# A packed-attention and channel-mix kernel: the second sequence's k is loaded ahead of w_k and transposed between warm-up products, w_r's first piece is loaded ahead of v, the ninth block of the first weights goes first

## The chip, the cores and the metric

The kernel runs on one core of one Trainium2 chip. The metric is device time in microseconds of one execution, the median of several runs. A profiled execution is looked at beside it: its span is the time from its first to its last instruction, and its own time is the device time of that one execution. The text calls TensorE PE, VectorE DVE, ScalarE ACT, GpSimd POOL and the queue of SyncE, from which nearly all transfers are issued, SP.

## The reference, cut to what matters

```python
scale = 1.0 / np.sqrt(64)                       # q, k, v: (8, 8, 576, 64); p: (8, 8, 32, 64)
def sm_attn(qq, kk, vv):
    s = scale * np.matmul(qq, kk.transpose(0, 1, 3, 2))
    a = np.exp(s - np.max(s, axis=-1, keepdims=True))
    a = a / (np.sum(a, axis=-1, keepdims=True) + 1e-09)
    return np.matmul(a, vv)
p_packed = sm_attn(p, k, v)                     # 32 rows for each head
x = sm_attn(q, p_packed, p_packed)              # then (8, 576, 512): heads side by side
x_prev = x moved down by one row, its first row 0
xk = mu_k * x + (1.0 - mu_k) * x_prev
xr = mu_r * x + (1.0 - mu_r) * x_prev
kk = np.maximum(xk @ w_k, 0.0)                  # w_k (512, 1024), float64, as w_v and w_r
v = kk * kk @ w_v                               # w_v (1024, 512)
out = 1.0 / (1.0 + np.exp(-(xr @ w_r))) * v     # w_r (512, 512)
```

## The kernel before, in words

Eight sequences of 576 rows make 4608 rows of x; the channel mix takes them in nine blocks (NB) of 512 rows. For each block there are three chains of products on PE: the gates (xr @ w_r, written to `pr`), the keys (xk @ w_k, written to `ph`) and the values (squared keys @ w_v, written to `pvo`). Each operand is split into a high and a low part, so every product of 128x128 by 128x512 is done three times, in lines 1206 to 1208, 1158 to 1160 and 1236 to 1238; such a group of three is called a main group below.

The weights are float64 in memory. Each of the 4 pieces of w_r, 8 of w_k and 8 of w_v is loaded into an `st` buffer of 512 KB and converted in `convert`: ACT makes `m` (L297), DVE does three steps on it (L299, L301, L303), ACT casts the high part (L311), DVE subtracts to get the low part (L313).

The first sequence is treated in a way of its own. Its k, v and q are loaded as whole runs (`runs`), k is transposed on PE (L395) and copied by ACT (L398); `first_front` makes the scores (L548), DVE takes the row maxima (L642, L644), ACT the exponentials (`first_weights`, L646 and L651). The weights `a` are transposed in nine blocks (L568) into two PSUM tiles, `copied` brings them to `aT` (L632 for four blocks, L634 for the ninth), and nine times 16 products with v (L582) give the packed values, which DVE scales (`pm`, L600). They are transposed (L611), copied by ACT (`ppB`, L620), and `by_token` makes the second attention's scores with q (L927, L932); `weights_by_token` makes its softmax on DVE and ACT (`et`, lines 949 to 963), its transposes go to `A` (L976). `first_mix` multiplies A by pm, already weighed with mu (L1027), and ACT and DVE write the tiles xr and xk of the first block (L1043, L1052). The second sequence's k and q (`loads`, b < EARLY) are loaded with 96 rows to a tile, `raw`, and transposed on PE in `transposed_on_pe` (L479, six transposes to a pair of heads, 24 for k), ACT copies them (L482), and L670 makes the scores from them. The other sequences are transposed by DVE.

Nothing is ordered by hand. A planner, `Flow`, runs when the program is built: each part of the work is a generator that names the engine and a duration that the planner supposes, and at each step the part that could start first goes next, with its rank as the tie breaker. Ranks also decide who gets a buffer. What the planner decides is a fixed order of instructions on each engine, each queue working strictly in that order. Transfers are put in order by ranks too: `FIRST` holds those of the four pieces of w_r, `lrank` those of a sequence's k, v and q, `RANK_W` that of w_k. While it expects PE to be idle the planner puts in warm-up products, `fill` (L1342, tile `spare`), each of which shows in the trace as two passes; it stops that when the second part of the first block's gates begins. The buffers in play are `sq` (8, first v and q of the first sequence, later tiles of xr and squared keys), `raw` (3), `kq` (4), `st` (8) and two PSUM tiles `pa`.

Of the kernel before, what the change touches and what calls it, by code (L numbers as in the profile page):

```python
# [16 lines left out]
class Flow:  # L17
# [21 lines left out]
    def __init__(self):  # L39
        self.free = {"tensor": 1.4}  # L40
        self.parts = []
        self.n = 0
        self.now = None
        self.when = {}
        self.waiting = {}
        self.slots = {}
        self.table = "exp"
        self.warmth = 0.0
        self.keep_busy, self.fill = 0.0, None
# [73 lines left out]
    def order(self, part):  # L123

        start, ready = self.start(part)
        engine, table = part.want[0], part.want[3]
        if table and table != self.table and start - ready < self.PATIENCE:
            start += self.TABLE
        if part.last == (engine, part.t) and part.gen.__name__ in self.CHAINS:
            start = max(start - self.SAME, self.free.get(engine, 0.0))  # L130
        return start, part.rank, part.n
# [40 lines left out]
def attn_pack_channel_mix(ctx: ExitStack, tc: tile.TileContext, q, k, v, p, mu_k, mu_r, w_k, w_v, w_r, out):  # L172
    nc = tc.nc
# [21 lines left out]
    FIRST = 9.992, 10.06, 10.07, 10.08  # L195
    RANK_1, RANK_MIX, RANK_W, RANK_V, LOADS_1 = 14.28, 11.5, 13.6, 15.2, 14.29
# [69 lines left out]

    warm = const.tile([P, 1], F32, name="warm")
# [58 lines left out]
    def loads(b):  # L326
        flow.spawn(packed(b), lrank(b) - 0.03)
        for src, tag in ((k, "kT"), (v, "vt"), (q, "qT")):
# [7 lines left out]
            flow.now.rank = lrank(b) - (0.02 if tag == "kT" else 0.0)  # L336
            for pr in range(NPR):

                slot = yield from flow.take("raw")
                if b < EARLY:  # L340

                    raw = tile_([P, 6, 2 * D], F32, "raw", slot, "raw")
                    for hh in range(2):
                        yield from load(
                            raw[:T6, :, hh * D:(hh + 1) * D], src[b, 2 * pr + hh].rearrange("(c p) d -> p c d", p=T6),
                            0.5, 0.62,
                        )
                        back_to_issue()
                    flow.spawn(transposed_on_pe(tag, b, pr, slot, raw), rank(b), flow.free["dma"] + LANDS)
                    continue  # L350

# [9 lines left out]
                flow.spawn(transposed(tag, b, pr, slot, raw), rank(b), flow.free["dma"] + LANDS)  # L361

# [106 lines left out]
    def transposed_on_pe(tag, b, pr, raw_slot, raw):  # L469
# [10 lines left out]
        flow.give("raw", raw_slot)  # L480
# [55 lines left out]
    def first_front():  # L536
# [28 lines left out]
        for o, n, copy in ((0, 4, act), (4, 4, act), (8, 1, act)):  # L565
# [10 lines left out]
        for o, n in ((0, 4), (4, 4), (8, 1)):  # L576
            yield from flow.wait(("aT", 0, o), *(("vt", 0, pr) for pr in range(NPR)))
            yield pe(0.13 * n)
            for j in range(o, o + n):
                for pr in range(NPR):  # L580
                    for h, own in enumerate(HALVES):
                        nc.tensor.matmul(  # L582
                            pv[32 * pr:32 * pr + 32, h, :D], aT[own, j, 32 * pr:32 * pr + 32],
                            vts[0, pr][1][own, j * D:(j + 1) * D], start=(j == 0), stop=(j == RUN - 1),
                        )
# [601 lines left out]
    def gates(i):  # L1187

        for tiles in ((0,), (1, 2, 3)) if i == 0 else ((0, 1), (2, 3)) if i == 1 else ((t,) for t in range(NT)):
            slots, prs = [], []  # L1190
            if i == 0:
                yield from flow.wait(*made("xr", i, 0, tiles[0]))
                if tiles[0]:
                    flow.keep_busy = 0.0
                    flow.give("m", 3)
            for x in tiles:
# [26 lines left out]
    def values(i):  # L1223
        slots, pv = {}, {}
        for f in range(NF):
            yield from flow.wait(("sq", i, f), *(("wv", f, o) for o in range(0, DM, WP)))
            sf, hl = sqs.pop((i, f))
            for t in range(NT):
# [7 lines left out]
                nc.tensor.matmul(pv[t], sh, wvs[f][:, 0, :], start=(f == 0), stop=False)  # L1236
                nc.tensor.matmul(pv[t], sh, wvs[f][:, 1, :], start=False, stop=False)  # L1237
                nc.tensor.matmul(pv[t], sl, wvs[f][:, 0, :], start=False, stop=(f == NF - 1))  # L1238
                if f == NF - 1:
                    flow.spawn(done(i, t, slots[t], pv[t]), 0, flow.t + flow.LAG)  # L1240
            flow.give("sq", sf)

    def done(i, t, slot, pv):
        yield from flow.wait(("sig", i, t))
        sg, sig = sigs.pop((i, t))
        yield vec(DM)
# [94 lines left out]
    def fill():  # L1341
        nc.tensor.matmul(spare[:, :P], ident, ident, start=True, stop=True)  # L1342
# [28 lines left out]
```

## Time and profile before

| what | value |
|---|---|
| median of three runs | 591.75 us |
| the profiled execution's own time | 591.73 us |
| its span | 589.6 us |
| PE busy | 579.4 us (98% of the span), 4119 products |
| DVE busy | 371.8 us (63%) |
| ACT busy | 316.4 us (54%) |
| bytes read from and written to HBM | 43.00 MB and 12.98 MB |

Of the three runs 591.61 is the lowest; one, at 1153.4 us, stands apart. The profiled execution's own time is 2.1 us over its span; the table's busy times are of the span. Products are pipelined and the trace's durations of them overlap, so PE's busy time is above the time that it needs; the distance from one start to the next tells that.

### The profile page before, as it was taken

The page shows a single profiled execution, that of the slowest core. Times are in us where ns is not written, and L with a number is a line of the kernel's source. Part 1 is how long each engine was busy: PE and PEld are TensorE (multiplying, and loading weights), DVE is VectorE, ACT ScalarE, POOL GpSimd, SP SyncE. Part 2 cuts the span into 40 slices and gives each one's busy share as a digit, 9 for nine tenths or more (in the row PEclk, how much of TensorE's full clock was granted, in tenths as well). Part 3 has the DMA queues.
Part 4 walks back from the last instruction along what each step waited for, and adds up shares of the span by engine and source line. Part 5 has one row for each costly group of instructions (what it writes and reads, how often), then busy time and mean ns, then how long its engine had stood idle before and what let it go on. Part 6 is the DMA issues. An engine that isn't in the chain of part 4 may idle for free.

```text
span 589.6 us, 10544 instructions
## 1 busy us (share of the span) xinstructions
PE 579.4 (98%) x4119; PEld 457.2 (78%) x4119; DVE 371.8 (63%) x702; ACT 316.4 (54%) x571; POOL 7.8 (1%) x33
## 2 busy tenths in 40 slices
PE   8999999999999999999999999999999999999997
PEld 7877777787687778778778777878788888888885
DVE  1899889856892897289876697379214712541321
ACT  4678984764753692287456475358335613721410
POOL 3000000000000000000000000000000000000000
PEclk9999999999999999999999999999999999999999
DMA  8887340863556176346466444400100010001001
GB/s 304 334 231 238 114 65 10 190 141 59 127 118 146 25 155 139 91 112 138 78 183 135 83 101 117 116 2 0 73 0 1 0 73 0 1 0 72 1 1 71
DMA packets 160593, 56.66 MB, mean 96 GB/s; under 512 B 136856, under 2 KB 150304, under 8 KB 160544
## 3 DMA queue, kind: packets, MB, share of 16 engines
q1 hardware_dynamic: 160224, 55.86, 37.4%
q8 instruction: 32, 0.52, 0.4%
q0 software_dynamic: 320, 0.14, 0.1%
q14 instruction: 17, 0.14, 0.1%
HBM read 43.00 MB, written 12.98 MB: 95 GB/s over the span
## 4 chain that ended last, share of the span: by engine, by line
PE 74%; DVE 16%; ACT 5%; issue 2%; DMA 1%; SPq 1%; DVEq 0%; ACTq 0%
PE ph L1158 10%; PE ph L1159 9%; PE ph L1160 9%; PE pvo L1236 9%; PE pvo L1237 8%; PE pvo L1238 8%; PE pr L1206 5%; PE pr L1208 5%; PE pr L1207 5%; DVE x L1113 2%; PE pa L894 2%; DVE m L301 2%; PE pa L704 1%; DMA q<-in_q 1%; PE pa L670 1%
## 5 line engine op out<-in xcount | busy, mean ns | idle before, releaser
L1158 PE MATMUL ph<-xk,wk_h 128*128 128x512 f32 x288 | 115.5, 401 | 0.0
L1236 PE MATMUL pvo<-wv,sq 128*128 128x512 f32 x288 | 113.9, 396 | 0.0
L1159 PE MATMUL ph<-xk,wk_h 128*128 128x512 f32 x288 | 112.4, 390 | 0.0
L1160 PE MATMUL ph<-xk,wk_l 128*128 128x512 f32 x288 | 112.2, 390 | 0.0
L1237 PE MATMUL pvo<-wv,sq 128*128 128x512 f32 x288 | 112.2, 390 | 0.0
L1238 PE MATMUL pvo<-wv,sq 128*128 128x512 f32 x288 | 112.1, 389 | 0.0
L1169 ACT ACTIVATE r<-ph 128x512 f32<-128x512 f32 x72 | 43.2, 600 | 86.5 <-PE ph L1160 84.4
L1180 DVE CAST sq<-r 128x512 fp32r<-128x512 f32 x64 | 26.9, 421 | 97.1 <-ACT r L1172 93.6
L1236 PEld LDWEIGHTS pvo<-wv,sq 128*128 128x128 f32 x288 | 54.1, 188 | 16.3 <-issue 5.4
L1158 PEld LDWEIGHTS ph<-xk,wk_h 128*128 128x128 f32 x288 | 54.0, 188 | 16.3 <-issue 5.4
L1160 PEld LDWEIGHTS ph<-xk,wk_l 128*128 128x128 f32 x288 | 54.1, 188 | 11.5
L1238 PEld LDWEIGHTS pvo<-wv,sq 128*128 128x128 f32 x288 | 54.1, 188 | 11.4
L1237 PEld LDWEIGHTS pvo<-wv,sq 128*128 128x128 f32 x288 | 54.1, 188 | 10.6
L1159 PEld LDWEIGHTS ph<-xk,wk_h 128*128 128x128 f32 x288 | 54.2, 188 | 10.1 <-DVE xk L1052 0.2
L1206 PE MATMUL pr<-wr_h,xr 128*128 128x512 f32 x144 | 57.5, 399 | 0.3 <-ACT xr L1133 0.3
L1208 PE MATMUL pr<-wr_h,xr 128*128 128x512 f32 x144 | 56.2, 390 | 0.3 <-DVE xr L1135 0.3
L1207 PE MATMUL pr<-wr_l,xr 128*128 128x512 f32 x144 | 56.2, 390 | 0.0
L1113 DVE SCALAR_TENSOR_TENSOR x<-xt,mus,x 128x448 f32<-128x448 f32 (+6 forms) x112 | 52.7, 510 | 4.8 <-ACT x L1107 4.8
L1107 ACT ACTIVATE x<-xt,mus 128x448 f32<-128x448 f32 (+7 forms) x112 | 54.2, 529 | 1.2 <-DVE xr L1135 1.2
L1182 DVE TENSOR_TENSOR sq<-r,sq 128x512 fp32r<-128x512 f32 x72 | 49.2, 683 | 4.7 <-ACT sq L1177 3.3
L1218 ACT ACTIVATE sig<-pr 128x512 f32<-128x512 f32 x36 | 20.9, 600 | 55.3 <-PE pr L1208 55.1
L1247 DVE TENSOR_TENSOR sig<-pvo,sig 128x512 f32<-128x512 f32 x36 | 24.0, 685 | 37.3 <-PE pvo L1238 37.2
(151 smaller groups left out, 707.6 us busy)
## 6 DMA issues: line engine op xcount, KB each, us to landing
out<-sig SPq DMA_DIRECT2D x31, 256.0 KB, 2.6
vt<-in_v SPq DMA_DIRECT2D x14, 512.0 KB, 4.8
raw<-in_k SPq DMA_DIRECT2D x96, 72.0 KB, 2.7
raw<-in_q SPq DMA_DIRECT2D x96, 72.0 KB, 2.7
st<-in_moe_w_k SPq DMA_DIRECT2D x8, 512.0 KB, 8.5
st<-in_moe_w_v SPq DMA_DIRECT2D x8, 512.0 KB, 5.0
far<-at SPq DMA_DIRECT2D x12, 288.0 KB, 2.8
aTd<-far SPq DMA_DIRECT2D x12, 256.0 KB, 3.0
```

The lines of the kernel that those rows point to most:

```text
L1107: nc.scalar.mul(x32[:, o:o + n], xts[b, c][:, 1 + s:1 + s + n], mus[:, j, c:c + 1])
L1113: nc.vector.scalar_tensor_tensor(x32[:, o:o + n], xts[b, c][:, s:s + n], mus[:, j + 1, c:c + 1], x32[:, o:o + n], op0=ALU.mult, op1=ALU.add,)
L1158: nc.tensor.matmul(ph, wk_h[:, c, fs], xh, start=(c == 0), stop=False)
L1159: nc.tensor.matmul(ph, wk_h[:, c, fs], xl, start=False, stop=False)
L1160: nc.tensor.matmul(ph, wk_l[:, c, fs], xh, start=False, stop=(c == NC - 1))
L1182: nc.vector.tensor_tensor(hl[:, 1, :], r, hl[:, 0, :].bitcast(F32), op=ALU.subtract)
L1206: nc.tensor.matmul(pr, xh[:, ts_], wr_h[:, c, :], start=(c == 0), stop=False)
L1207: nc.tensor.matmul(pr, xh[:, ts_], wr_l[:, c, :], start=False, stop=False)
L1208: nc.tensor.matmul(pr, xl[:, ts_], wr_h[:, c, :], start=False, stop=(c == NC - 1))
L1236: nc.tensor.matmul(pv[t], sh, wvs[f][:, 0, :], start=(f == 0), stop=False)
L1237: nc.tensor.matmul(pv[t], sh, wvs[f][:, 1, :], start=False, stop=False)
L1238: nc.tensor.matmul(pv[t], sl, wvs[f][:, 0, :], start=False, stop=(f == NF - 1))
```

## The change

Six edits are made. The planner holds PE free from 0.5 instead of 1.4, and the warm-up products take a tile of zeros, set by DVE at the start, in place of the identity, which POOL makes. The ranks put w_r's first piece ahead of v, and the second sequence's k (`K_1`) ahead of w_k; that k is now loaded into buffers of `sq` rather than `raw` (`whole`). In `first_front` the ninth block is transposed and multiplied first. `copied` is preferred by 0.6 in the planner's choice. The very last main group of the last block is cut into two halves of 256 columns, and so are its multiplication by the gate and its write. Buffer `a` has one slot fewer until the second part of the first gates.

```diff
-        self.free = {"tensor": 1.4}
+        self.free = {"tensor": 0.5}
...
+        if part.gen.__name__ == "copied":
+            start = max(start - 0.6, self.free.get(engine, 0.0))
...
-    FIRST = 9.992, 10.06, 10.07, 10.08
-    RANK_1, RANK_MIX, RANK_W, RANK_V, LOADS_1 = 14.28, 11.5, 13.6, 15.2, 14.29
+    FIRST = 9.985, 10.05, 10.06, 10.07
+    K_1, RANK_1, RANK_MIX, RANK_W, RANK_V, LOADS_1 = 10.08, 14.28, 11.5, 13.6, 15.2, 14.29
...
+    flow.slots["a"].pop()
+    zeros = tile_([P, P], F32, "a", 1, "zeros")
+    nc.vector.memset(zeros, 0.0)
...
+            if b < EARLY:
+                if tag == "kT":
+                    flow.spawn(whole(src, tag, b), K_1)
+                else:
+                    yield from whole(src, tag, b)
+                continue
...
+    def whole(src, tag, b):
+        space = "sq" if tag == "kT" else "raw"
+        for pr in range(NPR):
+            slot = yield from flow.take(space)
+            raw = tile_([P, 6, 2 * D], F32, space, slot, "raw")
+            for hh in range(2):
+                yield from load(
+                    raw[:T6, :, hh * D:(hh + 1) * D], src[b, 2 * pr + hh].rearrange("(c p) d -> p c d", p=T6),
+                    0.5, 0.62,
+                )
+                back_to_issue()
+            flow.spawn(transposed_on_pe(tag, b, pr, space, slot, raw), rank(b), flow.free["dma"] + LANDS)
...
-        for o, n, copy in ((0, 4, act), (4, 4, act), (8, 1, act)):
+        for o, n, copy in ((8, 1, act), (0, 4, act), (4, 4, act)):
...
-        for o, n in ((0, 4), (4, 4), (8, 1)):
+        for o, n in ((8, 1), (0, 4), (4, 4)):
...
+                halves = 2 if i == NB - 1 and t == NT - 1 and f == NF - 1 else 1
+                for o in range(0, DM, DM // halves):
+                    cols = slice(o, o + DM // halves)
+                    nc.tensor.matmul(pv[t][:, cols], sh, wvs[f][:, 0, cols], start=(f == 0), stop=False)
...
+        if halves == 2:
+            for o in range(0, DM, DM // 2):
+                cols = slice(o, o + DM // 2)
+                yield vec(DM // 2)
+                nc.vector.tensor_tensor(sig[:, cols], pv[:, cols], sig[:, cols], op=ALU.mult)
+                yield from load(out[i * TB + t * P:i * TB + t * P + P, cols], sig[:, cols], 0.63, 0.4)
+                back_to_issue()
+            return
...
-        nc.tensor.matmul(spare[:, :P], ident, ident, start=True, stop=True)
+        nc.tensor.matmul(spare[:, :P], zeros, zeros, start=True, stop=True)
```

Line numbers after the change are 12 to 25 higher. The rows that follow give the order of instructions on an engine, before and after; a name is the tile that is written and those that are read.

DVE's first instructions before, up to pm (`mx` the first sequence's row maxima, `m` the first piece of w_r in conversion):

```order
L642 TENSOR_REDUCE mx<-pa 128x1
L644 TENSOR_SCALAR nmx<-mx 128x1
L642 TENSOR_REDUCE mx<-pa 128x1
L644 TENSOR_SCALAR nmx<-mx 128x1
L299 TENSOR_SCALAR m<-m 128x512
L301 SCALAR_TENSOR_TENSOR m<-st,m 128x512
L303 SCALAR_TENSOR_TENSOR m<-st,m 128x512
L594 SCALAR_TENSOR_TENSOR rs<-sm 128x2
L596 RECIPROCAL rs<-rs 128x2
L600 TENSOR_TENSOR pm<-pa,rs 128x256
L313 TENSOR_TENSOR wr_l<-m,wr_h 128x512
```

The same stretch of DVE after:

```order
L271 MEMSET zeros 128x128
L304 TENSOR_SCALAR m<-m 128x512
L654 TENSOR_REDUCE mx<-pa 128x1
L656 TENSOR_SCALAR nmx<-mx 128x1
L654 TENSOR_REDUCE mx<-pa 128x1
L656 TENSOR_SCALAR nmx<-mx 128x1
L306 SCALAR_TENSOR_TENSOR m<-st,m 128x512
L308 SCALAR_TENSOR_TENSOR m<-st,m 128x512
L318 TENSOR_TENSOR wr_l<-m,wr_h 128x512
L606 SCALAR_TENSOR_TENSOR rs<-sm 128x2
L608 RECIPROCAL rs<-rs 128x2
L612 TENSOR_TENSOR pm<-pa,rs 128x256
```

The whole conversion of w_r's first piece now stands ahead of pm, and its first DVE step ahead of the row maxima; the ACT step that it waits for (`m<-st`) moved ahead of the first exponentials likewise.

ACT between the last exponential of the first weights and the copies `ppB`, before (`aT` are the copies of the nine blocks, `t` the PSUM tile of the ninth, `qT` the copies of q's transposes):

```order
L651 ACTIVATE a_215,sm<-pa,nmx 128x64
L417 COPY qT<-pq 128x512
L297 ACTIVATE m<-st 128x512
L417 COPY qT<-pq 128x512
L632 COPY aT_277<-pa 128x512 x2
L417 COPY qT<-pq 128x512 x2
L634 COPY aT_277<-t_276 128x128
L311 CAST wr_h<-m 128x512
L297 ACTIVATE m<-st 128x512 x2
L620 COPY ppB<-pa 64x256 x2
```

The same stretch of ACT after:

```order
L663 ACTIVATE a_216,sm<-pa,nmx 128x64
L316 CAST wr_h<-m 128x512
L429 COPY qT<-pq 128x512
L646 COPY aT_291<-t_290 128x128
L644 COPY aT_291<-pa 128x512 x2
L429 COPY qT<-pq 128x512 x2
L302 ACTIVATE m<-st 128x512
L429 COPY qT<-pq 128x512
L632 COPY ppB<-pa 64x256 x2
```

The ninth block's copy moved from behind four copies of qT to behind one, the first piece's cast moved ahead of all of them, and ahead of `ppB` there stands one step of a conversion instead of two.

PE from the third group of second-attention scores to the third main group, before (`tpt` the transposes of the second attention's weights, `raw` the second sequence's k):

```order
L932 MATMUL s2t<-ppB,qT 64x32 x8
L1342 MATMUL spare<-ident 128x128 x2
L969 MATMUL tpt<-ident,et 128x2x64 x4
L1342 MATMUL spare<-ident 128x128 x3
L1027 MATMUL pa<-A_421,pms 64x192 x16
L1342 MATMUL spare<-ident 128x128 x5
L1206 MATMUL pr<-wr_h,xr 128x512
L1207 MATMUL pr<-wr_l,xr 128x512
L1208 MATMUL pr<-wr_h,xr 128x512
L479 MATMUL pa<-ident,raw 128x96 x3
```

The same stretch of PE after:

```order
L944 MATMUL s2t<-ppB,qT 64x32 x8
L491 MATMUL pa<-ident,raw 128x96 x6
L981 MATMUL tpt<-ident,et 128x2x64 x4
L491 MATMUL pa<-ident,raw 128x96 x6
L1367 MATMUL spare<-zeros 128x128 x7
L1039 MATMUL pa<-A_426,pms 64x192 x16
L981 MATMUL tpt<-ident,et 128x2x64 x4
L1367 MATMUL spare<-zeros 128x128 x2
L1219 MATMUL pr<-wr_h,xr 128x512
L1220 MATMUL pr<-wr_l,xr 128x512
L1221 MATMUL pr<-wr_h,xr 128x512
L491 MATMUL pa<-ident,raw 128x96 x12
```

Twelve of k's 24 transposes now stand ahead of the first main group and twelve right behind it; before, six stood in these early gates and eighteen between the main groups of the first keys. On ACT two copies of kT and the last exponential of the second attention's weights came to stand ahead of the four casts of xr; before, none of the four kT copies stood there. In the whole program 36 warm-up products are left of 43, and 16 of ACT's table loads of 18.

## Rows read from the trace of the kernel before

**Rows 1.** The page's first part: busy time of each engine in us, share of the span, number of instructions.

```profile
PE 579.4 (98%) x4119; PEld 457.2 (78%) x4119; DVE 371.8 (63%) x702; ACT 316.4 (54%) x571; POOL 7.8 (1%) x33
```

**Rows 2.** Busy time by stretch: the stretch, its length, busy us and instructions of PE, PEld, DVE, ACT, POOL, then the granted clock of TensorE, DMA share, GB/s.

```profile
20.00:30.00 10.00, 9.62 (x148) 8.73 (x147) 9.65 (x22) 4.88 (x12) 1.17 (x4) 1.00 0.78 272
30.00:40.00 10.00, 9.91 (x147) 7.92 (x145) 9.72 (x25) 6.59 (x18) 0.00 (x0) 1.00 0.78 208
40.00:50.00 10.00, 10.00 (x159) 7.74 (x160) 9.69 (x22) 8.59 (x18) 0.10 (x1) 1.00 0.86 296
50.00:62.00 12.00, 11.86 (x89) 8.53 (x88) 11.83 (x24) 11.42 (x23) 0.00 (x0) 1.00 0.71 204
62.00:80.00 18.00, 17.53 (x107) 14.09 (x109) 13.38 (x26) 17.21 (x33) 0.00 (x0) 1.00 0.36 89
80.00:113.00 33.00, 32.03 (x261) 23.44 (x253) 32.27 (x58) 20.01 (x44) 0.10 (x1) 1.00 0.39 83
```

**Rows 3.** The same view for the warm-up products alone: busy us and passes of PE and PEld, clock, DMA.

```profile
30.00:40.00 10.00, 2.83 (x20) 2.17 (x18) 1.00 0.78 208
40.00:580.00 540.00, 0.00 (x0) 0.00 (x0) 1.00 0.35 82
```

**Rows 4.** Timeline of the first 21 us, rows of PE, ACT and DVE in order of time: start, us, engine, line, operation, tiles, count, and in brackets the idle time before and what ended it.

```profile
2.43 2.50 PE L1342 MATMUL spare<-ident 128*128 128x128 f32 x10 [2.43 <-POOL ident masks.py:199]
...
9.94 1.50 PE L548 MATMUL pa<-kT,pt 64*32 64x320 f32 x32
10.94 0.82 DVE L642 TENSOR_REDUCE mx<-pa 128x1 f32<-128x640 f32 x1 [10.94 <-PE pa L548]
...
13.57 0.66 PE L411 MATMUL pq<-ident,q 128*128 128x128 f32 x4 [0.16 <-DMA q<-in_q]
13.88 0.21 ACT L651 ACTIVATION_READ_ACCUMULATOR a<-pa,nmx 128x1 f32 x1
...
14.80 0.68 ACT L297 ACTIVATE m<-st 128x512 f32<-128x512 f32 x1
14.84 1.04 PE L568 MATMUL pa<-ident,a 128*128 128x128 f32 x8
15.52 0.43 DVE L299 TENSOR_SCALAR m<-m 128x512 uint32<-128x512 uint32 x1 [2.64 <-ACT m L297]
15.92 1.08 ACT L632 COPY aT<-pa 128x512 f32<-128x512 f32 x2
15.98 0.69 DVE L301 SCALAR_TENSOR_TENSOR m<-st,m 128x512 uint32<-128x512 uint32 x1
16.88 1.09 ACT L417 COPY qT<-pq 128x512 f32<-128x512 f32 x2
17.00 1.66 PE L582 MATMUL pa<-v,aT 64*32 64x64 f32 x144
17.83 0.31 ACT L634 COPY aT<-t 128x128 f32<-128x128 f32 x1
18.70 0.42 DVE L600 TENSOR_TENSOR pm<-pa,rs 128x256 f32<-128x256 f32 x1 [1.03 <-PE pa L582]
19.70 0.75 ACT L620 COPY ppB<-pa 64x256 f32<-64x256 f32 x2
```

**Rows 5.** Transfers: issues of k and v on SP (timeline: start, us, count), time from issue to landing of v's four and, last, of w_k's first piece, issued at 12.83; then the time at which ACT first reads w_k.

```profile
3.16 1.86 SPq L219 DMA_DIRECT2D v<-in_v x4
...
DMA to landing us min/median/max: 6.1/6.5/7.0
...
DMA to landing us min/median/max: 8.2/8.2/8.2
...
33.79 0.69 ACT L297 ACTIVATE m<-st 128x512 f32<-128x512 f32 x1
```

**Rows 6.** Timeline of 50 to 62 us: PE's main groups of the first keys, the transposes of the second sequence's k, that sequence's scores; DVE's low parts of xk; ACT's copies of kT.

```profile
50.10 0.39 PE L1158 MATMUL ph<-xk,wk_h 128*128 128x512 f32 x1
53.78 0.39 PE L1159 MATMUL ph<-xk,wk_h 128*128 128x512 f32 x1
54.24 0.66 PE L479 MATMUL pa<-ident,raw 96*128 96x96 f32 x6
54.68 0.47 PE L1158 MATMUL ph<-xk,wk_h 128*128 128x512 f32 x1
55.45 0.41 PE L479 MATMUL pa<-ident,raw 96*128 96x96 f32 x3
59.94 1.20 PE L670 MATMUL pa<-kT,pt 64*32 64x288 f32 x32
...
52.66 0.48 DVE L1052 TENSOR_TENSOR xk<-pa,xk 128x320 fp32r<-128x320 f32 x1
...
53.45 0.68 ACT L482 COPY kT<-pa 128x576 f32<-128x576 f32 x1
```

**Rows 7.** The end: the last rows of the chain that ended last (start, us, what), the writes by size (count, KB, median us to landing), and a row of warm-up passes at 19.45.

```profile
585.31 0.23 PE pvo L1237
585.54 0.24 PE pvo L1238
585.80 0.69 DVE sig L1247
...
out<-sig SPq DMA_DIRECT2D x31, 256.0 KB, 2.6
out<-sig SPq DMA_DIRECT2D x10, 128.0 KB, 2.4
...
19.45 1.28 PE L1342 MATMUL spare<-ident 128*128 128x128 f32 x10
```

**Rows 8.** Who waited for whom on PE over the whole span: us in total, times, longest; behind it, the row of the same view of 40 to 62 us for a wait of the first keys on DVE.

```profile
PE pa L894 <- DVE a L886: 1.8, 4, 0.8
PE pr L1208 <- DVE xr L1135: 0.3, 1, 0.3
...
PEld ph L1159 <- DVE xk L1052: 0.2, 1, 0.2
```

**Rows 9.** Timeline of 29 to 32 us: the last exponential of the second attention's weights and the four casts of xr on ACT, the first main product on PE.

```profile
29.20 0.42 ACT L954 ACTIVATE et<-et 64x256 f32<-64x256 f32 x1
29.52 0.99 ACT L1043 CAST xr<-pa 128x192 fp32r<-128x192 f32 x4
...
30.55 0.48 PE L1206 MATMUL pr<-wr_h,xr 128*128 128x512 f32 x1
```

## What the change should do to the time

> **What bounds the kernel now.** I read the page's busy shares first, then busy time by stretch, then the timeline of the opening, then the chain of waits at the end. PE is busy 98% of the span [rows 1]; that says little, since warm-up products count and overlapping products count twice. By stretch the reader is to see two regimes [rows 2]. From 113 us on, PE runs main groups back to back, and the waits on PE that the whole span shows are a few us [rows 8]; nothing in the diff touches that part except the very end. Ahead of that DVE decides: from 20 to 62 us it works 40.9 of 42 us, while PE is padded with warm-up products up to 40 us and with none after [rows 3]. From 62 to 80 ACT is full (17.2 of 18) and DVE is not (13.4), from 80 to 113 DVE is full again (32.3 of 33). So the change can gain in three places: how early DVE's full stretch begins, what PE and ACT still have to do between 50 and 62, and the tail. The granted clock is 1.00 in all these rows, the level of 2.4 GHz.
>
> All sums are made against the profiled execution's own time, 591.73 us, of which 589.6 are its span; the median of the runs is 591.75, so the two can be taken as one.
>
> **The opening: 0.4 us earlier.** What starts DVE's full stretch is the chain scores, maxima, exponentials, transposes, products with v, pm, ppB [rows 4]. PE starts its first warm-up product at 2.43, when POOL has made the identity; the zeros come from DVE, idle until 10.94, so k can be transposed up to 1.5 us earlier, and the scores, at 9.94 now, may come near 9. That alone gives nothing, because in the new order the maxima wait on DVE behind the first step of w_r's first piece, and that piece has to land. It takes the place of v in the queue. v's four transfers are issued at 3.16 to 4.6 and land 6.1 to 7.0 us later, that is 9.3 to 11.6, one every 0.77 us for 288 KB [rows 5]. A piece of 512 KB counts as 1.8 of them: 9.3 + 0.8 x 0.77 = 9.9. Then ACT's step (0.68) and DVE's first (0.43) [rows 4] put the maxima at about 11.05, where they stood at 10.94. The exponentials end 3.15 us later as before (13.88 + 0.21 against 10.94), at 14.2.
>
> The gain comes after that. Before, the transposes of the weights stand behind two tiles of q and start at 14.84; now behind one, whose products begin at 13.57 and end at 14.2, so all nine are done by 15.3. ACT then casts w_r (DVE is through its two further steps of 0.7 at 14.4; the cast as long as ACT's other step) until 15.05, copies one qT (0.55), the ninth block (0.31) and the eight others (1.08): 17.0, as before. But the ninth block no longer ends the chain. Before, its copy stood behind two qT and began at 17.83, and the products with v ended at 18.66; now only the last four blocks' 64 of 144 products follow at 17.0, 0.75 us, and pm comes at 17.8 instead of 18.70. Of these 0.9 us half is given back: ACT has two more qT, a conversion step and a fourth qT to do before ppB, 17.0 + 1.1 + 0.68 + 0.55 = 19.3, against 19.70. So 0.4 us. Bounds: with w_r landing where v's first does, 9.3, it is 1.0; where v's last does, 11.6, it is -1.3. I take the middle row's pace.
>
> DVE's work from there to 62 us is the same work in another order, and it has no idle time to give up in which the order could matter; the shift of 0.4 stays.
>
> **Loads moved past each other.** v lands up to 1.4 us later, by 13.0; its first use moves from 17.00 to about 16, so it is covered. The eight loads of k (1.15 MB) pass w_k on SP; their buffers are v's, free only after the products with v at 17.8, so SP holds everything behind them until then. Both directions have room: w_k's first piece lands at 12.83 + 8.2 = 21.0 and is first read at 33.79 [rows 5]; three us later costs nothing. pin, v and q of the second sequence come behind and are not needed before 59 us.
>
> **k's transposes and copies: 1.7 us.** Before, eighteen of the 24 transposes stand between main groups of the first keys. From the first such group at 50.10 to the scores at 59.94 are 9.84 us [rows 6]. By the order eleven main groups lie in them, three products of 0.23 us each from start to start [rows 7], so 7.5. The remaining 2.35 us are transposes with their switches and waits. Now these transposes stand where PE ran warm-up products (by the order, 26 of these from 18 us on before, 16 after) and cost it nothing there. Not all of it is gained, because part of that stretch is DVE's: the fourth low part of xk is made from 52.66 to 53.14, and the group that reads it cannot pass before that [rows 6]. From there to the end of the transposes at 55.65 PE loses 0.6 (53.78 instead of 53.15) and 0.7 (54.24 to 54.68, and 55.45 to 55.65 with a slow start after it): 1.3 us is gained even if DVE is no earlier relative to its own shift. With the new order, in which the four low parts stand in one row on DVE, up to the whole 2.35. Zero is the other bound: if w_k's last low parts, DVE's work, become what every group waits for. I take 1.7, nearer to 1.3 because DVE has next to no idle time there.
>
> ACT must keep up: three copies of kT, 0.68 us each or some 0.54 from start to start (two of aT take 1.08 [rows 4]), leave this stretch (11.4 of 12 us busy) for 25 to 35 us, where ACT has five idle. That is 1.6 us off ACT, which is what the ACT-bound stretch to 80 needs to start 1.7 earlier; DVE has 4.6 idle there. From 80 to 113 DVE's full stretch starts earlier by as much and carries the shift to PE.
>
> **The tail: 0.3 us.** The last product ends at 585.78, DVE's multiplication takes 0.69, then the write [rows 7]. Of half the size the multiplication takes 0.42 (pm's, 128x256 [rows 4]): 0.27 gained. A write of 128 KB lands in 2.4 us, one of 256 KB in 2.6: at most 0.2. The six half products cost between 0.112 each, the distance of warm-up passes of 128 columns (1.28 for ten, the last one's drain included), and 0.23, that is 0.67 to 1.36 instead of 0.68; I take 0.15 more. Sum 0.3, bounds -0.4 and 0.5.
>
> The Trainium skill, TensorE: Matmul & The Clock Gate, section Back-to-back issue gap, gives 262 cycles for 256 columns, an estimate of 0.109 us; by it the six cost nothing and the term is 0.45; no row of before has products of 256 columns. The Trainium skill, DMA: Bandwidth & Descriptors, section Rules for kernel authors, advises against cutting a transfer into two halves since they serialize on the same engines; it speaks of partition halves, but by it the smaller write gains nothing and the term is 0.1; the medians of [rows 7] stand against it with 0.2, and no write here was cut in two.
>
> **After 113 us: nothing, give or take 1.** The orders of all later blocks come out a little different. The waits that could vanish are those of [rows 8]; as many can appear.
>
> Sum: 0.4 + 1.7 + 0.3 = 2.4, so 591.73 - 2.4 = 589.3 us.
>
> **The rivals.**
>
> DVE stays the bound. The transposes leave PE but the main groups only wait for w_k's low parts instead. For it: DVE is busy 11.83 of 12 us. Against it: PE shows a wait on DVE of only 0.2 us there [rows 8], though with the transposes there to fill. It leaves the opening and the tail: 591.0.
>
> The order suits the later stretches too. In the two stretches up to 113 the part of DVE's 4.6 idle us that ACT caused is used, and the waits of [rows 8] go: about 2 us more, 587.2.
>
> Slower: the second attention's chain on ACT. The last exponential of `et` stood at 29.20 and the four casts of xr at 29.52 behind it; the first main product came at 30.55 [rows 9]. In the new order a copy of kT and that exponential stand ahead of the casts, and the exponential waits for a DVE step that now comes behind the second group's maxima, sums and product, five steps and about 2.5 us. Counted through, the casts come near 31.4 and the first main product 1.7 us late. PE makes up for it only if it then runs without a pause, which it did not before (2.8 us of warm-up products between 30 and 40 [rows 3]). If it does not, and DVE bounds 50 to 62 too, the sum is 0.4 + 0.3 - 1.7: 592.7. It decides if the first main product comes after about 32 and the gates end later than 50.1.
>
> The change does not do what it says: k's loads wait for v's buffers and hold SP so long that w_k's later pieces or the transposes come late. The 12 us of room in [rows 5] speak against it; 592 or more.
>
> **How the numbers follow.** Forecast 0.54, DVE stays the bound 0.2, later stretches too 0.13, ACT's chain 0.1, loads late 0.03. The range: the largest terms together (1.0 + 2.35 + 0.5, and 1.0 of the later waits) give 586.9, the smallest without the ACT rival (0.4 + 0 - 0.4, and 0.5 of new waits) 592.2; I widen the low end to 586.7. That leaves out about a tenth, half of it above. 2% of this time, 11.8 us, is about what a measurement of this kernel can tell from no change; nothing here comes near it: faster by more 0.01, within 0.98, slower by more 0.01.
>
> **What would show it.** The maxima on DVE start between 10.6 and 11.5, pm's multiplication near 17.8, ppB's copies near 19.3. No kT copy on ACT after 40 us, and the second sequence's scores on PE near 58 instead of 59.94. PE's last product ends about 2 us earlier than at 585.78. I am wrong if w_r's first piece lands after 11, if PE shows waits for w_k's low parts between 52 and 62, or if the shift at 60 us is there and gone at 115.

## The result, and the profile after

The changed kernel takes 595.52 us, the median of five runs (593.7 to 596.11), the kernel before 591.61 in the runs beside it: a ratio of 1.0061, with an interval of 1.0051 to 1.0072. It is slower by 3.9 us where 2.4 us less were forecast, and outside the range. The profiled execution is the quickest of the five, 593.7 us with a span of 591.6; what its trace shows, 2.0 us more than before, is about half of the loss; the four slower executions left no trace.

Busy time by stretch, as in [rows 2], of the changed kernel (columns: stretch, its length, busy time of PE, its weight loads, DVE, ACT and POOL with instructions, granted clock, DMA share, GB/s):

```profile
20.00:30.00 10.00, 9.73 (x152) 8.96 (x151) 9.72 (x23) 5.47 (x10) 0.00 (x0) 1.00 0.94 266
30.00:34.70 4.70, 2.32 (x22) 1.61 (x14) 4.44 (x13) 3.03 (x8) 0.00 (x0) 1.00 1.03 293
36.00:40.00 4.00, 4.00 (x55) 2.19 (x54) 2.08 (x4) 2.13 (x5) 0.00 (x0) 0.57 0.79 226
40.00:50.00 10.00, 9.72 (x161) 7.02 (x153) 7.98 (x19) 7.70 (x19) 0.00 (x0) 1.00 1.01 289
50.00:62.00 12.00, 12.00 (x126) 9.89 (x108) 11.63 (x23) 10.43 (x22) 0.10 (x1) 1.00 0.53 164
```

DVE, which was full from 20 to 62 us in [rows 2], has idle time now: 2.08 of 4 us busy from 36 to 40, 7.98 of 10 from 40 to 50. In the same place PE has 2.4 us without work (30 to 34.7), and behind it the granted clock averages 0.57 for four microseconds, that is, PE runs at 1.2 GHz for most of them. Neither is in the kernel before.

The opening went better than forecast. Timeline of DVE and ACT of the changed kernel, beside [rows 4]:

```profile
9.94 0.82 DVE L654 TENSOR_REDUCE mx<-pa 128x1 f32<-128x640 f32 x1
...
17.96 0.42 DVE L612 TENSOR_TENSOR pm<-pa,rs 128x256 f32<-128x256 f32 x1 [3.12 <-PE pa L594]
...
19.01 0.74 ACT L632 COPY ppB<-pa 64x256 f32<-64x256 f32 x2
```

The maxima start 1.0 us earlier than before, pm and ppB 0.7. What follows is PE from 30 to 41 us; it answers to [rows 9], where the first main product came at 30.55:

```profile
30.95 0.47 PE L1219 MATMUL pr<-wr_h,xr 128*128 128x512 f32 x1
...
32.13 0.44 PE L491 MATMUL pa<-ident,raw 96*128 96x96 f32 x3 [0.25 <-issue]
34.76 0.93 PE L491 MATMUL pa<-ident,raw 96*128 96x96 f32 x9 [2.19 <-DMA raw<-in_k]
35.48 0.48 PE L1219 MATMUL pr<-wr_h,xr 128*128 128x512 f32 x1
...
37.55 0.63 PE L1220 MATMUL pr<-wr_l,xr 128*128 128x512 f32 x1
...
38.54 2.31 PE L1039 MATMUL pa<-A,pms 32*64 32x256 f32 x96
```

Behind the first main group stand twelve transposes of the second sequence's k, the third and the fourth pair of heads in turn, three at a time. The third pair's first three run; the next three belong to the fourth pair, and its data is still on its way: 2.19 us of waiting for `raw`. So all nine that are left, and every main product behind them, wait. ACT stands in the same line: the copies of kT wait for the transposes, and w_r's cast stands behind them:

```profile
32.28 1.24 ACT L302 ACTIVATE m<-st 128x512 f32<-128x512 f32 x2
35.49 1.18 ACT L494 COPY kT<-pa 128x576 f32<-128x576 f32 x2 [1.98 <-PE pa L491]
37.07 0.27 ACT L988 COPY A<-tpt 128x128 f32<-128x128 f32 x1 [0.40 <-PE tpt L981]
37.23 0.62 ACT L316 CAST wr_h<-m 128x512 fp32r<-128x512 f32 x1
```

DVE then waits 2.0 us for that cast. A product of 512 columns that takes 0.39 us elsewhere takes 0.60 to 0.79 from 36.0 to 38.5.

Why the pair is late is seen on SP, which issues the transfers in its fixed order (start, us, what, count); the second fence is the view of that line from 26.8 to 27.8 us, the time from issue to landing of the two loads there, of which the trace holds the landing of the second:

```profile
17.77 6.93 SPq L221 DMA_DIRECT2D raw<-in_k  x6
24.75 1.97 SPq L221 DMA_DIRECT2D st<-in_moe_w_k  x2
26.82 0.93 SPq L221 DMA_DIRECT2D raw<-in_k  x2
```

```profile
DMA to landing us min/median/max: 7.4/7.4/7.4
```

Six of k's eight loads go out together, then two pieces of w_k of 512 KB each, then the fourth pair's two loads, issued at 26.8 and 27.2, the second of which needs 7.4 us to land, up to 34.6. The DMA engines are busy meanwhile (share 1.03 from 30 to 34.7).

### The profile page after: what moved, and what is told of

It reads as the page before. It is cut to its first block, busy times and chain, and to the rows that moved or that the text cites. A ratio compares the mean times of both kernels' runs of the same rounds, so it can differ in the third digit from the quotient of the medians.

```text
span 591.6 us, 10533 instructions
## 1 busy us (share of the span) xinstructions
PE 579.2 (98%) x4108; PEld 455.6 (77%) x4108; DVE 370.7 (63%) x704; ACT 315.4 (53%) x569; POOL 7.8 (1%) x33
## 4 chain that ended last, share of the span: by engine, by line
PE 76%; DVE 12%; ACT 6%; DMA 3%; issue 2%; SPq 0%; DVEq 0%; ACTq 0%
PE ph L1170 9%; PE pvo L1253 9%; PE ph L1172 9%; PE ph L1171 9%; PE pvo L1255 9%; PE pvo L1254 9%; PE pr L1219 5%; PE pr L1221 5%; PE pr L1220 5%; DVE x L1125 2%; PE pa L716 2%; PE pa L906 1%; DMA q<-in_q 1%; DMA raw<-in_k 1%; PE pa L682 1%
## 5 line engine op out<-in xcount | busy, mean ns | idle before, releaser
L1192 DVE CAST sq<-r 128x512 fp32r<-128x512 f32 x64 | 26.8, 419 | 105.9 <-ACT r L1184 103.3
L1219 PE MATMUL pr<-wr_h,xr 128*128 128x512 f32 x144 | 58.0, 403 | 0.0
L1221 PE MATMUL pr<-wr_h,xr 128*128 128x512 f32 x144 | 56.9, 395 | 0.9 <-DVE xr L1147 0.6
L1184 ACT ACTIVATE r<-r 128x512 f32<-128x512 f32 x72 | 45.5, 632 | 1.8
```

The lines of the kernel that those rows point to most:

```text
L1219: nc.tensor.matmul(pr, xh[:, ts_], wr_h[:, c, :], start=(c == 0), stop=False)
L1221: nc.tensor.matmul(pr, xl[:, ts_], wr_h[:, c, :], start=False, stop=(c == NC - 1))
```

## The experiments

Two theories were set against each other. A: the loss comes of that one pair, whose loads stand behind two pieces of w_k while its transposes stand ahead of the gates, and of the clock's fall behind the wait. B: the early loads as such cost.

**k's loads together.** The cleanest test: on every engine but SP nothing moves. By the two traces PE's 4108 instructions, ACT's 569, DVE's 704 and POOL's 33 stand in the same order in both kernels.

```diff
+        own = []
+        for pr in range(NPR if tag == "kT" else 0):
+            own.append((yield from flow.take(space)))
         for pr in range(NPR):
-            slot = yield from flow.take(space)
+            slot = own[pr] if own else (yield from flow.take(space))
```

> The changed kernel, but the second sequence's k takes all four buffers before its first load, so that its eight loads follow each other. On PE, ACT, DVE and POOL every instruction stands where it stands in the changed kernel; on SP alone the fourth pair's two loads stand ahead of the two pieces of w_k that they stood behind. Theory A (the late fourth pair, its wait on PE and the fall of the clock): the fourth pair lands near 29 us in place of 34.63, the twelve transposes run through near 32.2 us, the second main product starts near 33.2 us, the granted clock stays at 1.00, and the time is that with the warm-up products less the wait that they stood in (0.8 us of wait and some 2 us of products): 589.5 to 590 us. Theory B (the early loads as such cost, by the later w_k): 592.5 us or above. Theory D (what is lost later, in the order of the work behind 60 us, as the kernel with the fourth pair's transposes put late shows): 593 to 595 us.

590.35 us, ratio 0.9978 (0.9969 to 0.9988). So the place of two loads on SP, with nothing else moved, is worth 5.2 us in the medians (4.9 by the two ratios), and the kernel passes from slower than before to quicker. Timeline of SP and of PE:

```profile
17.80 8.65 SPq L221 DMA_DIRECT2D raw<-in_k  x8
26.49 2.41 SPq L221 DMA_DIRECT2D st<-in_moe_w_k  x4
...
32.12 1.20 PE L494 MATMUL pa<-ident,raw 96*128 96x96 f32 x12 [0.24 <-issue]
33.10 0.48 PE L1222 MATMUL pr<-wr_h,xr 128*128 128x512 f32 x1
...
35.14 1.87 PE L1042 MATMUL pa<-A,pms 32*64 32x256 f32 x96
```

Busy time by stretch, in the columns shown above:

```profile
36.00:40.00 4.00, 3.62 (x88) 2.51 (x69) 3.68 (x8) 2.81 (x8) 0.00 (x0) 1.00 0.91 262
```

All twelve transposes run through, the clock is 1.00, the second main product comes 2.4 us earlier than in the changed kernel, and the second mixing (A by pm, 38.54 there) 3.4. The spans of the two traces differ by 3.3 (588.3 and 591.6). Theory A holds against B and D, which gave 592.5 us or above; the time is 0.35 above the upper end that A gave.

**Warm-up products in the wait.** Nine products of zeros into the fourth pair's own PSUM tile, ahead of its transposes.

```diff
+            if tag == "kT" and pr == 3 and hf == 0:
+                for _ in range(9):
+                    nc.tensor.matmul(pT[:, 1, :P], zeros, zeros, start=True, stop=True)
```

> The changed kernel with nine more 128x128 warm-up products ahead of the transposes of the fourth pair, so that PE is busy while it waits for that pair's loads; nothing else moves. Theory A with the clock as a part of the loss of its own: the transposes still start near 34.8 us, but the granted clock is 1.00 from 36 to 40 us (0.57 in the changed kernel) and the time falls by the 1.7 us of the profiled run to the 3.5 us that a mean clock of 0.994 over 593 us leaves room for: 592 to 593.8 us. If the clock's fall has another cause, or costs nothing beside the wait: 595 to 596 us.

592.52 us, ratio 1.0015 (1.0005 to 1.0024), in the range given for the clock as a part of its own. Timeline of PE, and busy time by stretch:

```profile
32.16 2.25 PE L492 MATMUL pa<-zeros 128*128 128x128 f32 x18
35.23 0.93 PE L494 MATMUL pa<-ident,raw 96*128 96x96 f32 x9 [0.82 <-DMA raw<-in_k]
```

```profile
36.00:38.00 2.00, 2.00 (x13) 1.11 (x11) 0.00 (x0) 1.92 (x4) 0.00 (x0) 1.00 1.04 258
```

The transposes start even later than in the changed kernel, and the time is 3.0 us less, since the clock stays at 1.00. So in the medians the 5.2 us divide into 3.0 for the clock and 2.2 (592.52 to 590.35) for the wait itself. The traces show less: their spans differ by 1.0 (591.6 and 590.6). The changed kernel's five runs have mean clocks of 0.997 (593.7 and 595.33 us) or 0.994 (595.52 to 596.11), the kernel with these products 0.999 or 1.00. Only the quickest of the five was traced, and the run of 595.33 has its mean clock without its time; so the mean clock does not tell the whole spread, and the size of 3.0 rests on the medians alone.

**The fourth pair in a buffer of its own.**

```diff
+                    own = yield from flow.take("raw")
...
+            if own is not None and pr == 3:
+                space, slot = "raw", own
+            else:
+                slot = yield from flow.take(space)
```

> The changed kernel, but the fourth pair of k of the second sequence is loaded into a buffer of `raw` that is kept for it, so that its two loads stand right behind the third pair's and ahead of the fourth to last pieces of w_k. Theory A (the loss comes from the fourth pair, whose two loads stand behind two pieces of w_k, land at 34.63 us and hold PE for 2.2 us in its fixed order, and from the fall of TensorE's clock that follows): no wait of PE for raw near 32 to 35 us, the second main product near 32.5 us in place of 35.48, granted clock 1.00 from 36 to 40 us in place of 0.57, time 590 to 591.5 us. Theory B (the early loads as such cost: w_k comes later and ACT has the copies of kT among the casts of xr, whatever pair 4 does): the wait goes but the time stays at 594 us or above.

607.87 us, far from either. What A says of 32 us came true: no wait for `raw`, the second main product at 32.55. But the buffer taken away changed the planner's order of all that follows; the second sequence's scores now stand at 48.44, ahead of the last mixing of the first block, and PE waits for their exponentials. Who waited for whom on PE from 40 to 70 us (us in total, times, longest), and busy time by stretch:

```profile
PE pa L1043 <- ACT a L790: 7.4, 1, 7.4
PE ph L1174 <- ACT xk L1059: 1.7, 1, 1.7
```

```profile
50.00:62.00 12.00, 4.60 (x22) 3.43 (x26) 11.69 (x23) 9.20 (x16) 0.00 (x0) 0.84 0.60 205
62.00:80.00 18.00, 14.68 (x185) 11.02 (x177) 17.45 (x32) 14.00 (x30) 0.10 (x1) 0.73 0.25 46
```

As a test of A against B by time it is void, since more than one thing moved.

**The fourth pair's transposes late.**

```diff
+            late = 8.0 if tag == "kT" and pr == 3 else 0.0
-            flow.spawn(transposed_on_pe(...), rank(b), flow.free["dma"] + LANDS)
+            flow.spawn(transposed_on_pe(...), rank(b), flow.free["dma"] + LANDS + late)
```

> The changed kernel with the same order of loads (the fourth pair of k still behind two pieces of w_k), but the planner is told that the fourth pair lands 8 us later, so that its six transposes stand on PE behind the first gates' products and no longer ahead of them. Theory A (it is the place of these transposes in PE's fixed order that turns a late load into a stall and a slower clock): the second main product near 32.5 us in place of 35.48, granted clock 1.00 throughout 30 to 50 us, and time below the 590.41 us of the kernel without the k edit, by up to the 1.7 us that 18 transposes and their copies cost between 50 and 60 us: 588.7 to 590.4 us. Theory B (the early loads as such cost, by the later w_k): 592.5 us, as with the warm-up products, or above.

594.75 us, a miss for A by time, although each of its marks is there: the second main product at 32.24, clock 1.00 from 30 to 50 us, the second sequence's scores at 59.10, as early as the 59.30 of the kernel with the loads together. The 4.4 us between these two are lost behind 60 us, in the other order that the planner made there. Who waited for whom on PE over the whole span; four rows, all of them behind 60 us, that neither before nor the kernel with the loads together has in this size:

```profile
PE pvo L1255 <- DVE wv L318: 1.0, 1, 1.0
PE pa L492 <- ACT a L787: 0.9, 1, 0.9
PE pa L746 <- DVE pm L740: 0.8, 1, 0.8
PE pr L1220 <- ACT xr L1146: 0.8, 1, 0.8
```

They are 3.5 of the 4.4 us; the rest is not accounted for.

**The parts.** All edits but k's:

```diff
-                if tag == "kT":
-                    flow.spawn(whole(src, tag, b), K_1)
-                else:
-                    yield from whole(src, tag, b)
+                yield from whole(src, tag, b)
...
-        space = "sq" if tag == "kT" else "raw"
+        space = "raw"
```

> The changed kernel with the second sequence's k loaded as before (into `raw`, at its old rank): the other five edits alone. Theory A: the opening's gain (pm at 17.96 us in place of 18.70) and the halved end (0.25 us) both stand and nothing is lost near 32 us: 590.4 to 591.0 us. Theory C (an earlier opening is taken back by the loads and ACT behind it, so only the end remains): 591.3 us.

590.41 us, ratio 0.9980 (0.9971 to 0.9989): as A said. The k edit alone, on the kernel before:

```diff
+    K_1 = 10.08
...
+            if b < EARLY:
+                if tag == "kT":
+                    flow.spawn(whole(src, tag, b), K_1)
+                else:
+                    yield from whole(src, tag, b)
+                continue
```

> The kernel before with the k edit alone (K_1 and `whole`, buffers of `sq`): opening, warm-up products and end are as before. Here the order puts all eight loads of k behind four pieces of w_k and ahead of the other four. Theory A: the fourth pair lands near 29 us, no long wait near 32 us, and 18 transposes less are left for 50 to 60 us: 590 to 591.6 us. Theory B (the move of k costs by itself): 593.5 us or above.

589.8 us, ratio 0.9978 (0.9962 to 0.9994), 0.2 below the range of A; the quickest version of this study, though by medians within 0.6 us of the two at 590.4. Eight of its ten runs lie between 589.46 and 590.36, two at 593.81 and 592.32 with mean clocks of 0.993 and 0.996. The traced one is the slowest of the ten; the same kernel once more, for the trace of a quick execution:

> The kernel before with the k edit alone, a second time and for its trace: the profiled execution of the first time took 593.8 us at a mean clock of 0.993, eight of its ten runs 589.5 to 590.4 us at 1.00. If the clock's fall follows a wait of PE for k's first pair, as in that trace (1.6 us up to 28.37 us, 0.50 from 28 to 34 us), a run near 589.7 us shows no wait of that length, a granted clock of 1.00 from 26 to 36 us, and the first main product some 4 us before the 35.84 us of that trace. If the wait is there all the same, at a clock of 1.00, the clock falls for another reason.

589.74 us, on another chip, where the one run of the kernel before took 593.2. PE's wait for k's first pair and the first main product, and the clock (busy time by stretch), first in the execution of 593.81 us, then in this one:

```profile
28.37 1.19 PE L486 MATMUL pa<-ident,raw 96*128 96x96 f32 x6 [1.58 <-DMA raw<-in_k]
35.84 0.47 PE L1213 MATMUL pr<-wr_h,xr 128*128 128x512 f32 x1
```

```profile
28.00:30.00 2.00, 1.63 (x10) 1.66 (x11) 0.61 (x2) 0.40 (x1) 0.00 (x0) 0.50 0.91 208
30.00:32.00 2.00, 2.00 (x12) 2.00 (x12) 1.41 (x3) 1.78 (x5) 0.00 (x0) 0.50 1.00 279
```

```profile
27.07 0.69 PE L486 MATMUL pa<-ident,raw 96*128 96x96 f32 x6 [0.41 <-DMA raw<-in_k]
31.97 0.48 PE L1213 MATMUL pr<-wr_h,xr 128*128 128x512 f32 x1
```

```profile
28.00:30.00 2.00, 2.00 (x26) 1.85 (x24) 1.90 (x5) 2.00 (x5) 0.00 (x0) 1.00 1.05 247
30.00:32.00 2.00, 2.00 (x43) 1.68 (x35) 1.77 (x6) 1.74 (x6) 0.00 (x0) 1.00 0.90 259
```

One program, one order: in the slower execution PE can begin the first pair only 1.3 us later, the clock falls, and the end is 4.1 us later; the eight quick runs on its own chip lie as far ahead of it. So the same trap lies in this version; by the mean clocks it shuts in two runs of ten, in the changed kernel in all five.

The opening's edits and the end, on the kernel before. First the ranks of w_r:

```diff
-    FIRST = 9.992, 10.06, 10.07, 10.08
+    FIRST = 9.985, 10.05, 10.06, 10.07
```

> The kernel before with the new ranks of w_r's pieces alone (its first piece ahead of v). By the prediction this carries the opening's term, 0.4 us: 591.3 us. If the opening's whole measured gain (1.34 us between before and the kernel without the k edit) comes of it: 590.4 us. If it comes of the zeros, the ninth block and the preference for `copied`: 591.7 us.

591.33 us (0.9983 to 1.0001): the 0.4 of the prediction in the median, though the interval takes in no change.

The same with the ninth block and the preference:

```diff
+        if part.gen.__name__ == "copied":
+            start = max(start - 0.6, self.free.get(engine, 0.0))
...
-        for o, n in ((0, 4), (4, 4), (8, 1)):
+        for o, n in ((8, 1), (0, 4), (4, 4)):
```

> The kernel before with w_r's first piece ahead of v, the ninth block first and the preference for `copied`; warm-up products, k and the end as before. The first of these edits alone gave 591.33 us, all edits but k's 590.41 us. If the ninth block and the preference carry what lies between (0.7 us after 0.2 for the end): 590.6 us. If the zeros and the earlier start of PE carry it: 591.3 us.

590.99 us (0.9978 to 0.9996), against 591.85 of before in that series: 0.9 for three of the edits. The zeros and the end carry the rest of the 1.3; which of the two, these intervals do not tell.

The halved end:

```diff
+                halves = 2 if i == NB - 1 and t == NT - 1 and f == NF - 1 else 1
```

> The kernel before with the halved last main group alone. By the prediction 0.3 us less than before. By the traces of before and after nothing: from the first of the last three full products to the last landing there are 3.61 us in the kernel before (584.92 to 588.53) and 3.61 us in the changed one (587.04 to 590.65), since DVE's first half starts only behind the second half's products.

591.54 us (0.9987 to 1.0005), no change. Timeline of the end of the changed kernel, beside [rows 7]:

```profile
587.04 0.28 PE L1253 MATMUL pvo<-wv,sq 128*128 128x256 f32 x1
587.15 0.28 PE L1254 MATMUL pvo<-wv,sq 128*128 128x256 f32 x1
...
587.63 0.28 PE L1255 MATMUL pvo<-wv,sq 128*128 128x256 f32 x1
587.95 0.76 DVE L1267 TENSOR_TENSOR sig<-pvo,sig 128x256 f32<-128x256 f32 x2
```

The first half's three products end by 587.55 (the third starts at 587.27), but DVE takes the first half at 587.95, after the sixth product: both halves wait for PE's last one. Six half products from start to start are 0.71 us against 0.68 for three whole ones, and the two multiplications take 0.76 against 0.69. The split gives back all that it gains.

Two edits together, k's and the new ranks of w_r:

```diff
-    FIRST = 9.992, 10.06, 10.07, 10.08
+    K_1, FIRST = 10.08, (9.985, 10.05, 10.06, 10.07)
```

> The kernel before with two edits: the k edit (589.8 us alone) and w_r's first piece ahead of v (0.4 us alone). If the edits add up: 589.4 us. If each new start of the opening gives the planner another order and with it a time of its own, as the changed kernel against its parts suggests: anything from 588 to 596 us, and then a place in the trace, a wait on PE or a stretch at the lower clock, must show it.

591.66 us (0.9995 to 1.0013): the edits do not add up. Why is open, since the other nine runs, 591.25 to 592.63 us, have a mean clock of 0.999 or 1.00 and none of them was traced. The trace, of the slowest execution (593.92 us), shows the trap once more: PE waits 0.60 us for k's first pair up to 28.11, the clock is 0.57 from 28 to 32 us, and the first main product comes at 35.24.

## Why the prediction was wrong

**The step that failed is "Loads moved past each other".** It asked what the moved loads do to those that they pass, and found 12 us of room for w_k. It did not ask when k's own eight loads land, nor when PE, in its fixed order, wants them. The next term, that the transposes "stand where PE ran warm-up products [...] and cost it nothing there", needed that answer: a transposition costs nothing in a gap only if its data is there. The order of SP was to be had beforehand: two pieces of w_k between the third pair and the fourth, and PE's order with the fourth pair right behind the first main group. The order alone does not yet say that PE waits. With the third pair landed at 28.06, two pieces at the 1.25 us that they take in the trace of before, and two loads of k at the 0.5 us at which the others land behind each other, the fourth pair is there at about 31.6 us (an estimate), 1.0 ahead of PE, which is free for it at 32.57. That 1.0 us, and not the 12, was the room. The pieces took 2.0 and 2.3 us, and the pair's loads as much as 2.3 behind them: 34.6. The rival that named the event ("the transposes come late") got 0.03, since the room in [rows 5] was counted for the wrong transfer, and its price was left open at "592 or more".

**The clock was in no term.** All rows of before had 1.00, so a wait was priced at its own length. Of the 5.2 us the wait is 2.2 and the clock 3.0, by the medians.

**The opening: right in kind, too small.** w_r's first piece was put at 9.9 us; ACT reads it at 8.88, so it had landed ahead of even the lower bound, 9.3. The maxima came at 9.94 in place of 11.05, pm at 17.96 (17.8 forecast), ppB at 19.01 (19.3). All edits but k's are worth 1.3 us where opening and end were put at 0.7. One slip in the sum did no harm here: the upper end of the range took the opening at 0.4, though that term's own lower bound was -1.3, which gives 593.9 in place of 592.2.

**k's transposes: 1.7 us, there in both kernels, but given back in the changed one.** The term says that the first keys need less time without eighteen transposes among them. First and 48th product of the keys, first without the k edit (all edits but k's), then with it (k's loads together):

```profile
48.75 0.39 PE L1167 MATMUL ph<-xk,wk_h 128*128 128x512 f32 x1
...
63.02 0.39 PE L1169 MATMUL ph<-xk,wk_l 128*128 128x512 f32 x1
```

```profile
50.14 0.39 PE L1173 MATMUL ph<-xk,wk_h 128*128 128x512 f32 x1
...
63.09 0.39 PE L1175 MATMUL ph<-xk,wk_l 128*128 128x512 f32 x1
```

The stretch is 1.3 us shorter, near the term's 1.3 to 1.7, but it starts 1.4 later, so nothing is left (590.35 against 590.41). The loss is ahead of the keys: the first main product comes at 30.94 in place of 30.30, twelve transposes stand behind it in place of six among the first gates, and the second mixing starts at 35.14 in place of 33.86. On the kernel before, the k edit alone shortens the same stretch by 1.4 us (50.45 to 63.31, against 50.10 to 64.37) and starts it only 0.35 later; why the gates give back so much less there is open. Its 1.95 us in the medians, 1.3 by the ratio, agree with 1.7 partly by luck, since some 0.9 of the 2.0 us that its trace gains comes behind 63 us. The sign given for the term fails in both: the second sequence's scores start at 60.92 with the k edit alone, later than the 59.94 of before, and at 59.30 with the loads together (after 0.84 us of waiting for `pt` of DVE) against 58.59 without the k edit. So "near 58" was not a mark of k's transposes.

**ACT's chain, the rival at 0.1, did not decide.** The exponential did move behind (30.12), the casts came at 30.44 rather than 31.4, the first main product 0.4 us late in place of 1.7. With the k edit alone it came 1.4 us late (31.97), and that kernel was quicker all the same.

**The end: 0.3 forecast, 0 measured.** The half products' distance of 0.118 us was within the term's bounds. What was wrong is that the term took the first half's multiplication out of the path, which the wait for the last product puts back. The Trainium skill, TensorE: Matmul & The Clock Gate, section Back-to-back issue gap, had 262 cycles, an estimate of 0.109 us; the trace shows 0.118. The other page of the Trainium skill, DMA: Bandwidth & Descriptors, section Rules for kernel authors, led to "gains nothing" for the halved write; the trace differs on the write, whose last half lands in 1.8 us against 2.0 for a whole one (588.88 to 590.65, before 586.52 to 588.53). That 0.2 is lost again by the later issue and the longer multiplication.

**After 113 us: nothing, give or take 1.** For the changed kernel it is within that. Against the kernel before it is 2.7 us behind at the last value product of the first block (110.24 against 107.58) and 2.1 at the end of PE's last product (587.91 against 585.77). As a rule it was too narrow, as the late transposes show: against the kernel with the loads together they are 1.4 us behind at that value product (108.29 against 106.92), and 4.6 at the end of the span (592.9 against 588.3).

## What to carry to other kernels

When an order is fixed ahead of time, moving work into a gap moves it ahead of everything behind it: write down for each moved instruction when its data lands, by the queue's order as it now is, and what stands behind it. Price a wait on TensorE together with the clock that it may lose; here, by the medians, the clock was the greater part. Where a planner makes the order, a small edit is a new program: test it with all but the disputed instruction left in place, and do not add up the gains of parts.

## What was not expected of the hardware

A wait of 2.19 us on PE, up to 34.76, is followed by a granted clock of 0.51 from 36 to 38 us and 0.64 from 38 to 40, while PE is busy again (busy time by stretch, the changed kernel):

```profile
36.00:38.00 2.00, 2.00 (x7) 1.12 (x5) 0.11 (x1) 1.45 (x4) 0.00 (x0) 0.51 0.78 192
38.00:40.00 2.00, 2.00 (x50) 1.08 (x49) 1.97 (x4) 0.68 (x1) 0.00 (x0) 0.64 0.81 260
```

The same wait filled with 2.25 us of products leaves it at 1.00. In the kernel with the k edit alone a wait of 1.58 us is followed by 0.50, and one of 0.41 is not; with w_r's ranks beside it one of 0.60 is followed by 0.57.

The transfers of 512 KB that landed 1.25 us apart before (21.05 to 22.3 for two pieces of w_k) land 2.0 and 2.3 us behind the transfer ahead of them when they are issued among k's loads with their rows of 256 bytes (28.06, 30.07 and 32.35 in the changed kernel), at 256 to 315 GB/s from 30 to 36 us where 411 to 414 were moved from 10 to 20. What of this is the rows' size, and what the other transfers in the queue, was not tried.
